# A planned attention + gated-FFN kernel: q projections interleaved, gate matmuls queued later, a longer landing time in the planner, final waits sorted

## The chip, the cores and the metric

The kernel runs on one core of one Trainium2 chip. Times are device microseconds (us) of that core. Engines: PE is the TensorE matmul, PEld its weight load, DVE VectorE, ACT ScalarE, POOL GpSimd, SP the engine that issues nearly all DMAs; "SPq" and "ACTq" are issues by a sequencer.

## The reference, cut to what matters

```python
x = A_x                                             # 1 x 2048 x 512, bf16
g = sigmoid((x * gate_w).sum(-1, keepdims=True))
a = memory_attention(x, wq, wk, wv, wo, beta)       # 32 heads of 16, 4 segments of 512 tokens
b = (relu(x @ W_gate) * (x @ W_up)) @ W_down        # 512 -> 1792 -> 512
return g * a + (1 - g) * b
# memory_attention, for each segment s: masked softmax attention inside the segment, mixed with
#   phi(q) @ M / (phi(q) @ z);  then  M += phi(k)^T v,  z += sum phi(k);   phi(t) = t+1 if t>0 else exp(t)
```

Segment 0 needs no memory. The first update of M is needed by segment 1.

## The kernel before

The kernel contains its own planner. Every operation is declared with what it reads, what it writes and a guessed duration. A list scheduler then takes, on each engine, the ready operation of the best priority (the lowest number first), and so fixes the engines' orders; semaphore waits follow from the dependences. So a guess never makes a result wrong. It decides which instruction stands before which, and in a fixed order an instruction that must wait holds up everything behind it on its engine. Two terms: a warm-up matmul works on zeros and nobody reads its result, it keeps PE busy until x has landed; wq is loaded in four contraction tiles of 128 rows, each by a DMA of its own.

```python
# place(): the planner's guess of when a DMA lands
self.dma_busy = max(self.dma_busy, issued) + op.nbytes / 340.0
op.end = self.dma_busy + (1700.0 if start < 16000.0 else 3200.0)
...
# start: warm-up matmuls, then x of segment 0 is transposed on PE
ds.append(dve(lambda e: e.memset(V.rl[:, 0, :], 0.0), 300, writes=["rl0"], name="warm0"))
xps, xcs = [warm(6, 0, 3)], []
...
# x of the later segments comes by DMA transposes, behind all weights but wo and wd
load_gu(0); load_gu(1); load_x(1); load gwb; load wo; load wd        # (shortened)
...
# gate: gw_pe turns gate_w, gq["pe"] is gmm (16 tiny matmuls); "flex" are 16 small copies of the gate
# for each segment (gexpT), on DVE or ACT
sc.queue(2, [gw_pe] + gq["pe"])
sc.queue(2, gq["flex"])
...
# keys of a segment: ek = exp(k) on ACT, ek = phi(k) on DVE, phik = ek transposed by a DMA, then the update
acts.append(act(lambda e, G=G: e.activation(V.ek[:, G, :], V.kT[:, G, :], ACT.Exp), ..., reads=[f"kT{G}"], writes=[f"ek{G}"], name=f"kexp{s}_{G}"))
sbs.append(dve(lambda e, G=G: e.tensor_tensor(V.ek[:, G, :], V.ek[:, G, :], V.ttmp[:, G % 2, :], ALU.min), ..., name=f"kphi{s}_{G}"))
sps.append(dma("sp", lambda e, G=G: e.dma_start_transpose(V.phik[:, :, G * 128:(G + 1) * 128], V.ek[:, G, :]), ..., name=f"kT2{s}_{G}"))
pes.append(pe(fn, mm(160, 8), reads=[f"phik{2 * hf}", f"phik{2 * hf + 1}"] + va(s), name=f"mu{s}_{hf}", ep=ep, role="w"))
...
# the end: SP waits for the last DMA of each of 16 semaphores
for i in range(sc.ndma):
    if sc.cnt[f"dma{i}"]:
        sc.prog["sp"].append(("wait", f"dma{i}", 16 * sc.cnt[f"dma{i}"]))
```

There is one `ek` for all segments. The first exp of `ek` of segment 1 (kexp1_0) therefore waits until the transposing DMA of segment 0 (kT20_0) has read the old one.

The softmax here doesn't subtract the row's maximum and nothing guards it: scores larger than these inputs give would overflow.

## Time and profile before

| | before |
|---|---|
| time, median of the first 3 runs | 275.39 us (275.25 to 275.47) |
| span of the profiled run | 273.4 us |
| first matmul | 1.24 us |
| PE idle before the quad at 36.02 us | 0.87 us |
| end of the last matmul to end of the span | 2.79 us |

From the page of the kernel before: the span, the busy time of each engine (share of the span, number of instructions), and the chain of work that ended last, by engine.

```profile
span 273.4 us, 5333 instructions
PE 263.7 (96%) x2122; PEld 115.8 (42%) x2157; DVE 206.3 (75%) x402; ACT 198.4 (73%) x205; POOL 120.6 (44%) x167
PE 90%; DMA 4%; issue 2%; ACT 1%; DVE 1%; ACTq 1%
```

PE is the bound. A gain must come from time in which PE stands still.

From the timeline of the kernel before (start, duration, engine, line, operation, tiles; in brackets the idle time just before and what ended it):

```profile
26.60 5.19 SPq L603 DMA_TRANSPOSE phik<-ek  x3
...
33.57 0.63 ACT L600 ACTIVATE ek<-kT 128x512 bf16<-128x512 bf16 x1 [1.84 <-DMA phik<-ek]
...
34.07 0.47 PEld L623 LDWEIGHTS psA<-vaug,phik 128*128 128x128 bf16 x8 [0.52 <-DMA phik<-ek]
34.07 0.65 PE L623 MATMUL psA<-vaug,phik 128*128 128x136 bf16 x8
...
34.11 1.86 ACT L682 ACTIVATE E<-psL 128x2048 bf16<-128x2048 f32 x1
...
36.02 0.40 PE L677 MATMUL psL<-qT,kp 32*128 32x256 bf16 x8 [0.87 <-ACT E L682]
```

The transposes of `ek` are issued from 26.60 us. ACT waits 1.84 us for the first of them to land before it may overwrite `ek`. The exp of the logits behind it starts only at 34.11. It frees the PSUM banks that the next logits ("quad", L677) need, and PE waits 0.87 us for them.

The start, from the same view, where the change interleaves:

```profile
6.93 0.17 PE L514 MATMUL psA<-ident,g 4*128 4x4 bf16 x1
7.11 0.13 PEld L580 LDWEIGHTS psA<-xT,wq 128*128 128x128 bf16 x2
7.14 1.09 PE L580 MATMUL psA<-xT,wq 128*128 128x512 bf16 x4
...
7.61 0.13 PEld L580 LDWEIGHTS psA<-xT,wq 128*128 128x128 bf16 x2 [0.37 <-DMA wq<-in_A_wq_dram]
```

The prediction reads these four q matmuls as 1.09 us in place of 0.86. 1.09 runs from the first start to the last end, and each record is 0.38 us long, while the starts lie 0.22 us apart. Four that wait for nothing read 1.02 us in the same view (from the timeline of experiment 2's run, e_ek2):

```profile
7.28 1.02 PE L580 MATMUL psA<-xT,wq 128*128 128x512 bf16 x4
```

So the late second half of wq cost PE 0.07 us here, though the weight load waited 0.37. Before these four PE waits for the small gate load; counted from start to start that cost 0.18 us (0.49 us after the last warm-up matmul, 0.31 in e_dma, where nothing is waited for).

### The profile page before, as it was taken

The numbers are of one execution on the slowest core, as the hardware profiler recorded it, in microseconds if no ns is written. First come the engines' busy times: TensorE is split into PE (matmuls) and PEld (weight loads), VectorE is DVE, ScalarE is ACT, GpSimd is POOL, SyncE is SP. The second block draws the span as 40 slices with busy tenths as digits, with TensorE's granted clock in tenths as the row PEclk, the third lists the DMA queues.
The fourth block names the chain that finished last, engine by engine and source line by source line (L and its number), as shares of the span: only waits on it lengthen the run. The fifth ranks groups of instructions, "written<-read, shape, count | busy, mean of one in ns | idle before, by whom it ended". The sixth has DMA issues, their size and how long they took to land.

```text
span 273.4 us, 5333 instructions
## 1 busy us (share of the span) xinstructions
PE 263.7 (96%) x2122; PEld 115.8 (42%) x2157; DVE 206.3 (75%) x402; ACT 198.4 (73%) x205; POOL 120.6 (44%) x167
## 2 busy tenths in 40 slices
PE   8999989999999999999999999999999999999995
PEld 4433333434444444443434444444344343434444
DVE  5599979899999799999698968687863338688200
ACT  3498696888877897798668779977677678784122
POOL 4004975687637483754444464324233424241000
DMA  6997952111001235200013111000012000000011
GB/s 194 334 337 195 304 101 57 42 36 45 0 2 38 61 78 95 59 22 0 2 20 73 46 38 37 23 2 0 2 38 60 20 19 22 1 2 0 0 41 38
DMA packets 31025, 17.01 MB, mean 62 GB/s; under 512 B 20760, under 2 KB 31000, under 8 KB 31000
## 3 DMA queue, kind: packets, MB, share of 16 engines
q1 hardware_dynamic: 30416, 16.14, 23.3%
q10 hardware_dynamic: 584, 0.53, 0.7%
q8 instruction: 17, 0.28, 0.4%
q14 instruction: 8, 0.07, 0.1%
HBM read 9.84 MB, written 2.10 MB: 44 GB/s over the span
## 4 chain that ended last, share of the span: by engine, by line
PE 90%; DMA 4%; issue 2%; ACT 1%; DVE 1%; ACTq 1%
PE psA L747 35%; PE psA L786 18%; PE psL L677 9%; PE psA L580 8%; PE psA L702 7%; PE psA L578 5%; PE psA L779 5%; DMA phik<-ek 3%; DMA g<-in_gate_w_dram 2%; PE psA L652 1%; PE psA L623 1%; ACT E L682 1%; ACTq L414 1%; PE psA L639 0%; DVE ek L602 0%
## 5 line engine op out<-in xcount | busy, mean ns | idle before, releaser
L682 ACT ACTIVATE E<-psL 128x2048 bf16<-128x2048 f32 x80 | 150.0, 1875 | 33.6 <-PE psL L677 32.9
L685 POOL TENSOR_SCALAR_AFFINE_SELECT E<-E 128x512 bf16<-128x512 bf16 x128 | 86.1, 690 | 125.2 <-ACT E L682 125.1
L747 PE MATMUL psA<-xT,wg 128*128 128x512 bf16 x213 | 57.2, 380 | 1.7 <-issue 1.7
L747 PE MATMUL psA<-xT,wu 128*128 128x512 bf16 x218 | 58.0, 380 | 0.7 <-issue 0.5
L786 PE MATMUL psA<-wd,hT 128*128 128x512 bf16 (+1 forms) x230 | 53.5, 367 | 0.9 <-issue 0.6
L758 DVE TENSOR_TENSOR hT<-psA,rl 128x512 bf16<-128x512 f32 x56 | 38.3, 685 | 12.0 <-PE psA L747 11.0
L677 PE MATMUL psL<-qT,kp 32*128 32x384 bf16 (+3 forms) x512 | 31.7, 301 | 0.9 <-ACT E L682 0.9
L786 PEld LDWEIGHTS psA<-wd,hT 128*128 128x128 bf16 x238 | 21.6, 98 | 23.2 <-issue 3.6
L747 PEld LDWEIGHTS psA<-xT,wu 128*128 128x128 bf16 x224 | 20.4, 98 | 25.5 <-issue 2.9
L707 DVE STREAM_TRANSPOSE Tn<-psA 128x512 f32<-128x512 f32 x32 | 21.6, 700 | 12.4 <-PE psA L702 12.1
L747 PEld LDWEIGHTS psA<-xT,wg 128*128 128x128 bf16 x224 | 19.6, 98 | 24.7 <-issue 4.5
L596 POOL TENSOR_SCALAR kp<-kT,pm 128x512 bf16<-128x512 bf16 x15 | 24.6, 1640 | 1.3 <-DVE kT L593 1.0
L755 ACT ACTIVATE rl<-psA 128x512 bf16<-128x512 f32 x27 | 16.1, 596 | 11.9 <-PE psA L747 11.0
L756 DVE TENSOR_SCALAR rl<-psA 128x512 bf16<-128x512 f32 x29 | 19.8, 684 | 5.4 <-PE psA L747 4.5
L677 PEld LDWEIGHTS psL<-qT,kp 32*128 32x128 bf16 x512 | 8.9, 92 | 33.1 <-ACT E L682 19.2
L702 PE MATMUL psA<-E,vaug 128*17 128x256 bf16 (+3 forms) x512 | 21.0, 300 | 0.0
L796 ACT ACTIVATE osb<-psA,omg 128x512 bf16<-128x512 f32 (+1 forms) x12 | 7.8, 651 | 15.3 <-PE psA L779 13.3
L580 PE MATMUL psA<-xT,wq 128*128 128x512 bf16 x60 | 15.8, 379 | 0.6 <-issue 0.5
L779 PE MATMUL psA<-wo,oT 128*128 128x512 bf16 (+1 forms) x66 | 16.0, 366 | 0.3 <-issue 0.3
L580 PE MATMUL psA<-xT,wk 128*128 128x512 bf16 x62 | 15.5, 379 | 0.2 <-issue 0.2
L578 PE MATMUL psA<-wv,xT 128*128 128x512 bf16 x62 | 15.1, 380 | 0.3 <-issue 0.3
L702 PEld LDWEIGHTS psA<-E,vaug 128*17 128x17 bf16 x512 | 10.5, 90 | 10.8 <-issue 2.3
(75 smaller groups left out, 237.9 us busy)
## 6 DMA issues: line engine op xcount, KB each, us to landing
out_dram<-osb SPq DMA_DIRECT2D x15, 128.0 KB, 1.7
wg<-in_B_W_gate_dram SPq DMA_DIRECT2D x8, 224.0 KB, 5.4
wu<-in_B_W_up_dram SPq DMA_DIRECT2D x8, 224.0 KB, 6.1
wd<-in_B_W_down_dram SPq DMA_DIRECT2D x1, 1792.0 KB
osb<-in_A_x_dram SPq DMA_DIRECT2D x12, 128.0 KB, 2.1
wk<-in_A_wk_dram SPq DMA_DIRECT2D x4, 128.0 KB, 5.0
wv<-in_A_wv_dram SPq DMA_DIRECT2D x4, 128.0 KB, 4.4
wo<-in_A_wo_dram SPq DMA_DIRECT2D x1, 512.0 KB, 5.4
```

Of the source, the lines that this page charges most:

```text
L578: ins = e.matmul(A(ep)[:, :], lhsT=V.xT[:, kt, tok + col * 128:tok + (col + 1) * 128], rhs=w[:, kt, :], start=(kt == 0), stop=(kt == KT - 1))
L580: ins = e.matmul(A(ep)[:, :], lhsT=w[:, kt, col * 128:(col + 1) * 128], rhs=V.xT[:, kt, tok:tok + 512], start=(kt == 0), stop=(kt == KT - 1))
L596: km = lambda e, G=G, p=p, ks=ks: e.tensor_scalar(V.kp[:, ks, :], V.kT[:, G, :], V.pm[:, p:p + 1], None, ALU.mult)
L677: ins = q.matmul(PL[:, jj, o:o + w], lhsT=V.kp[32 * jj:32 * jj + 32, kslot(s, n), 128 * j:128 * j + 128], rhs=V.qT[32 * jj:32 * jj + 32, q ...
L682: acts.append(act(lambda a, e=e: a.activation(V.E[:, e, :, :], PL[:, :, :], ACT.Exp, scale=SCALE), t_act(2048), reads=[f"bankL{b}" for b i ...
L685: pools.append(pool(lambda g, ap=ap: g.affine_select(out=ap, in_=ap, compare_op=ALU.is_ge, fill=0.0, base=0, pattern=[[0, 4], [1, 128]], c ...
L702: ins = q.matmul(A(ep)[32 * jj:32 * jj + 17, c:512], lhsT=V.vaug[:, s % 2, j, 8 * G + 2 * jj + p, :], rhs=V.E[:, e, jj, o:o + w], start=(j ...
L707: ds.append(dve(lambda e, p=p, ep=eps[p]: e.transpose(V.Tn[:, p, :], A(ep)[:, :]), t_dve(512), writes=[f"Tn{p}"], name=f"tr{s}_{G}_{p}", e ...
L747: ins = e.matmul(A(ep)[:, :], lhsT=w[:, kt, f * 128:(f + 1) * 128], rhs=V.xT[:, kt, c * 512:(c + 1) * 512], start=(kt == 0), stop=(kt == K ...
L758: evs.append(dve(lambda e, ep=eu, r=r, hs=hs: e.tensor_tensor(V.hT[:, hs, :], A(ep)[:, :], V.rl[:, r, :], ALU.mult), t_dve(512), reads=[f" ...
L779: ins = e.matmul(A(ep)[:, 0:c1 - c0], lhsT=V.oT[:, o0 + G, i * 128:(i + 1) * 128], rhs=V.wo[:, G, c0:c1], start=st_ and G == 0, stop=sp_ a ...
L786: ins = e.matmul(A(ep)[:, 0:c1 - c0], lhsT=V.hT[:, slots[f], i * 128:(i + 1) * 128], rhs=V.wd[:, f, c0:c1], start=st_ and f == f0, stop=sp ...
```

## The change

The intent: the first two q projections interleaved by contraction tile as wq lands; the first memory update planned later; the final waits in order of landing. The diff also queues the gate matmuls at a lower priority. Cut to its core (the lines that only follow from the splitting and from the shorter memset are left out):

```diff
-            op.end = self.dma_busy + (1700.0 if start < 16000.0 else 3200.0)
+            op.end = self.dma_busy + (1700.0 if start < 16000.0 else 5200.0 if start < 60000.0 else 3200.0)
...
-    ds.append(dve(lambda e: e.memset(V.rl[:, 0, :], 0.0), 300, writes=["rl0"], name="warm0"))
+    ds.append(dve(lambda e: e.memset(V.rl[:, 0, 0:128], 0.0), 130, writes=["rl0"], name="warm0"))
...
-    xps, xcs = [warm(6, 0, 3)], []
+    xps, xcs = [warm(5, 0, 3)], []
...
-    sc.queue(2, [gw_pe] + gq["pe"])
+    sc.queue(3, [gw_pe] + gq["pe"])
...
-            for k0 in range(0, KT, 2):
+            step = 1 if s == 0 and name == "q" and col < 2 else 2
+            for k0 in range(0, KT, step):
...
             pes = [p for k in "qkv" for p in pes if p.name[0] == k]
+            pes[:2 * KT] = [pes[h * KT + kt] for kt in range(KT) for h in range(2)]
...
-    for i in range(sc.ndma):
+    for i in sorted(range(sc.ndma), key=lambda i: sc.dma_end.get(i, 0.0)):
```

More of the change, by code (lines that the diff above doesn't have):

```diff
@@ L481, in fn @@
             for i in range(n):
-                ins = e.matmul(PL[:, b, :], lhsT=V.rl[:, 0, 0:128], rhs=V.rl[:, 0, :], start=True, stop=True)
+                ins = e.matmul(PL[:, b, :], lhsT=V.rl[:, 0, 0:128], rhs=V.rl[:, 0, 0:128].unsqueeze(1).to_broadcast([128, 4, 128]), start=True, stop=True)
             return ins
         return pe(fn, n * (427 if k == 0 else 260), reads=["rl0"], writes=[f"bankL{b}"], name=f"warm{k}")
-    xps, xcs = [warm(6, 0, 3)], []
+    xps, xcs = [warm(5, 0, 3)], []
     for i in range(4):
@@ L572, in pj @@
             ep = Epoch("proj")
-            for k0 in range(0, KT, 2):
+            step = 1 if s == 0 and name == "q" and col < 2 else 2
+            for k0 in range(0, KT, step):
                 def fn(e, k0=k0):
-                    for kt in (k0, k0 + 1):
+                    for kt in range(k0, k0 + step):
                         if tokmajor:
@@ L581, in fn @@
                     return ins
-                pes.append(pe(fn, mm(512, 2), reads=[f"{wname}{k0}", f"{wname}{k0 + 1}"] + xt(s), name=f"{name}{s}_{col}", ep=ep, role="w2" if k0 else "w"))
+                pes.append(pe(fn, mm(512, step), reads=[f"{wname}{kt}" for kt in range(k0, k0 + step)] + xt(s), name=f"{name}{s}_{col}", ep=ep, role="w2" if k0 else "w"))
             return ep
```

## The prediction

> **What bounds it.** TensorE. The page gives a span of 273.4 us with PE busy 263.7 (96%); the chain that ended last is 90% PE. The matmuls stay but for one warm-up matmul, so the change can only win from the 9.7 us in which PE is idle. A table of 5 us stretches shows where: 1.24 us before the first matmul, 2.7 us after the last, 0.2 us in 5 to 10 us, 0.87 us in 35 to 40 us, and elsewhere bits of 0.16 us where matmuls change shape. Those bits stay.
>
> **What the change does.**
> 1. First projections. The timeline shows PE waiting 0.60 us for the small gate-weight load (until 6.93), then 4 q matmuls taking 1.09 us because later wq tiles landed late (weight load waited 0.37 us, until 7.61), then 16 tiny gate matmuls. Four steady projection matmuls take 0.86 us. With q0 and q1 interleaved, PE has four matmuls to do before the late tiles are needed, and the gate matmuls, at lower priority, no longer stand in front. Saved: 0.25 us at the late tiles and 0.1 to 0.2 us at the gate load. Given back: both q tiles finish together, one DVE copy is 0.69 us, and q2 waits for the first. Net 0.2 us.
> 2. Warm-up: a shorter memset (0.27 us before), 5 in place of 6 matmuls. The transposes then wait only for x (landed about 3.65) and start 0.1 us earlier, but wq's landing gates the projections. Worth 0. The Trainium skill (TensorE: Matmul & The Clock Gate, section "The HAM clock gate") says the clock opens after about 3.4 us of a busy, free-running window; the trace agrees in kind (warm-up matmuls are recorded at 634 ns early, 379 ns from about 6 us). If fewer matmuls move that, it costs some tenths.
> 3. The planner's DMA time for starts from 16 to 60 us grows by 2 us. In the trace the first phik transposes, issued at 26.60, landed after 6.95 us. The old plan (about 4.9 us) put the first memory-update matmuls, and an exp of ek that overwrites what the DMA still reads, too early: PE waited 0.52 us, ACT 1.84 us; the next exp of the logits started only at 34.11 and PE sat idle 0.87 us before the quad at 36.02. The new plan (6.9 us) puts other ready work there. But every other DMA in that stretch (phik's median is 2.4 us) is now planned too late, and every later choice of the list scheduler can fall differently. I count 0.6 us gained, with noise of half a us either way.
> 4. Final waits sorted by landing: the last DMA issue is at 271.20, the last SP wait ends about 273.0, the span at 273.4. Waits already met cost 20 to 30 ns each. Worth 0.1 us.
>
> **Sum.** 0.2 + 0 + 0.6 + 0.1 = 0.9 us off 275.39: **274.5 us**, range 273.5 to 275.5. Chances: faster by over 2% 0.01, within 2% 0.98, slower by over 2% 0.01.
>
> **What would show it.** (1) the timeline at 6.8 to 10 us: no wait on wq tiles, gate matmuls after the first eight; (2) clock opening still near 6 us; (3) in the waits, the memory-update weight load and the ek exp no longer wait for the phik DMA, and PE is busy about 4.8 of 5 us in 35 to 40; (4) a shorter stretch from the last landing to the end.
>
> **What would make it wrong.** The new order loses elsewhere: exps (the quads wait on them) pushed behind gate copies or relu; DVE, saturated from 12 to 30 us, delays the first key copies; phik lands later still; a later clock opening.

## The result, and the profile after

| | before | after |
|---|---|---|
| time, median of 6 runs | 275.43 us (274.58 to 275.75) | 274.28 us (273.85 to 274.54) |
| ratio of fast runs | | 0.996, 95% interval 0.9943 to 0.9976 |
| span of the profiled run | 273.4 us | 272.6 us |
| first FFN matmul (L747, L749 after) | 18.85 us | 18.58 us |
| end of the last matmul to end of the span | 2.79 us | 2.56 us |

A ratio is the mean time of one kernel's fast runs over that of the other's of the same rounds, so it is not quite the ratio of the medians. The kernel before scatters from 274.58 to 276.65 us over all rounds; a difference of 0.3 us between two kernels is hardly resolved by time alone, and the traces have to decide.

The lines of the page after that answer to those above:

```profile
span 272.6 us, 5368 instructions
PE 268.2 (98%) x2156; PEld 115.6 (42%) x2156; DVE 206.0 (76%) x421; ACT 192.9 (71%) x182; POOL 123.2 (45%) x171
PE 94%; DVE 3%; DMA 1%; ACT 1%; issue 0%; DVEq 0%
```

PE seems busier by 4.5 us, in a run shorter by 0.8. Most of that is the records: none are missing here. The Trainium skill (Perfetto Trace Analysis, section "Identifying the Most-Contended Engine") calls matmul busy time a bad measure of how close a kernel is to its roofline, because pipelined matmuls look smaller in the trace, and names MFU (the share of the peak rate that was used) and weight-load busy time as better ones. In this pair the weight loads stand at 42% both times, so they do not see the change at all; the stalls in the timeline do.

The same stretch of the timeline after, and the gate copies (gexpT) that have moved into it:

```profile
22.64 0.38 DVE L546 COPY gexpT<-gexp 32x4 f32<-32x4 f32 x1
25.34 0.90 ACT L547 ACTIVATE gexpT<-gexp 32x4 f32<-32x4 f32 x4
26.80 0.75 DVE L546 COPY gexpT<-gexp 32x4 f32<-32x4 f32 x4
...
30.31 0.41 DVE L603 TENSOR_TENSOR ek<-ek,ttmp 128x512 bf16<-128x512 bf16 x1
...
30.75 1.22 SPq L604 DMA_TRANSPOSE phik<-ek  x1
...
39.17 1.15 ACT L601 ACTIVATE ek<-kT 128x512 bf16<-128x512 bf16 x2
```

The first transpose is now issued at 30.75 and lands at 33.69 us by its semaphore, 2.94 us later (6.95 us before). So it lands no sooner than before (33.55). Both times it comes behind the load of W_down, issued at 22.35 and 22.52 us, whose last semaphore update comes at 33.06 and 33.19; from 30 to 31 us the DMAs move 349 GB/s in both. What has moved is who needs it: the exp that overwrites `ek` runs at 39.17 (33.57 before), the first memory update at 40.5 (34.07). Nobody waits. In windows (busy us and number of instructions of PE, PEld, DVE, ACT, POOL; then the clock, DMA share and GB/s), 30 to 31 and 33 to 38 us read, before:

```profile
30.00:31.00 1.00, 1.00 (x7) 0.44 (x5) 1.00 (x2) 1.00 (x1) 1.00 (x2) 1.00 1.11 349
33.00:38.00 5.00, 3.94 (x37) 1.81 (x31) 4.37 (x9) 4.43 (x5) 4.40 (x6) 1.00 0.78 130
```

and after:

```profile
30.00:31.00 1.00, 1.00 (x6) 0.39 (x4) 1.00 (x4) 0.94 (x1) 0.00 (x0) 1.00 1.10 349
33.00:38.00 5.00, 5.00 (x33) 1.94 (x32) 4.17 (x10) 4.47 (x6) 4.43 (x6) 1.00 0.75 90
```

A sum over the two profiled runs: the first FFN matmul comes 0.27 us sooner, the stall of 0.87 us is gone, the tail is 0.23 us shorter, and two new idle spells of PE stand at 85.19 us (0.21, shown below) and 129.7 us (0.12). That makes -1.04 us where the span shows -0.85. What makes up the other 0.19 us was not tested.

```profile
85.19 0.59 PE L641 MATMUL psA<-Mbd,phiq 128*128 128x8 bf16 x16 [0.21 <-DVE phiq L592]
```

### The profile page after: what moved, and what is told of

Read it like the earlier page. It is cut to its first block, busy times and chain, and to the rows that moved or that the text cites. A ratio compares the mean times of both kernels' runs of the same rounds, so it can differ in the third digit from the quotient of the medians.

```text
span 272.6 us, 5368 instructions
## 1 busy us (share of the span) xinstructions
PE 268.2 (98%) x2156; PEld 115.6 (42%) x2156; DVE 206.0 (76%) x421; ACT 192.9 (71%) x182; POOL 123.2 (45%) x171
## 4 chain that ended last, share of the span: by engine, by line
PE 94%; DVE 3%; DMA 1%; ACT 1%; issue 0%; DVEq 0%
PE psA L749 36%; PE psA L788 18%; PE psA L581 10%; PE psL L679 9%; PE psA L704 7%; PE psA L579 5%; PE psA L781 5%; DMA hT<-in_A_x_dram 1%; PE psA L654 1%; PE psA L625 1%; DVE gexpT L546 1%; PE psL L490 1%; ACT E L684 1%; PE psA L641 1%; DVE hT L760 1%; PE psL L482 0%
## 5 line engine op out<-in xcount | busy, mean ns | idle before, releaser
L687 POOL TENSOR_SCALAR_AFFINE_SELECT E<-E 128x512 bf16<-128x512 bf16 x128 | 83.1, 667 | 116.1 <-ACT E L684 113.0
L749 PE MATMUL psA<-xT,wu 128*128 128x512 bf16 x224 | 59.8, 380 | 0.0
L749 PE MATMUL psA<-xT,wg 128*128 128x512 bf16 x224 | 59.5, 380 | 0.1
L788 PE MATMUL psA<-wd,hT 128*128 128x512 bf16 (+1 forms) x238 | 54.6, 367 | 0.0
L597 POOL TENSOR_SCALAR kp<-kT,pm 128x512 bf16<-128x512 bf16 x19 | 30.7, 1620 | 2.6 <-PE psL L679 1.2
L749 PEld LDWEIGHTS psA<-xT,wu 128*128 128x128 bf16 x224 | 20.4, 98 | 25.4 <-issue 3.1
L749 PEld LDWEIGHTS psA<-xT,wg 128*128 128x128 bf16 x224 | 19.9, 98 | 24.7 <-issue 3.7
L758 DVE TENSOR_SCALAR rl<-psA 128x512 bf16<-128x512 f32 x28 | 19.0, 680 | 3.6 <-PE psA L749 2.9
L581 PE MATMUL psA<-xT,wq 128*128 128x512 bf16 x64 | 16.5, 380 | 0.0
L581 PE MATMUL psA<-xT,wk 128*128 128x512 bf16 x64 | 16.4, 381 | 0.0
L797 DVE TENSOR_SCALAR osb<-psA,omg 128x512 bf16<-128x512 f32 x8 | 6.0, 746 | 12.9 <-PE psA L788 12.9
L798 ACT ACTIVATE osb<-psA,omg 128x512 bf16<-128x512 f32 (+1 forms) x9 | 5.8, 639 | 13.7 <-PE psA L781 13.3
```

What stands on the lines that cost most here:

```text
L581: ins = e.matmul(A(ep)[:, :], lhsT=w[:, kt, col * 128:(col + 1) * 128], rhs=V.xT[:, kt, tok:tok + 512], start=(kt == 0), stop=(kt == KT - 1))
L597: km = lambda e, G=G, p=p, ks=ks: e.tensor_scalar(V.kp[:, ks, :], V.kT[:, G, :], V.pm[:, p:p + 1], None, ALU.mult)
L687: pools.append(pool(lambda g, ap=ap: g.affine_select(out=ap, in_=ap, compare_op=ALU.is_ge, fill=0.0, base=0, pattern=[[0, 4], [1, 128]], c ...
L749: ins = e.matmul(A(ep)[:, :], lhsT=w[:, kt, f * 128:(f + 1) * 128], rhs=V.xT[:, kt, c * 512:(c + 1) * 512], start=(kt == 0), stop=(kt == K ...
L788: ins = e.matmul(A(ep)[:, 0:c1 - c0], lhsT=V.hT[:, slots[f], i * 128:(i + 1) * 128], rhs=V.wd[:, f, c0:c1], start=st_ and f == f0, stop=sp ...
```

## The experiments

Two ways of editing were used. "Planned anew" means that a part of the change is put in or left out and the planner runs again. "Order kept" means that the planner's order is written out again instruction for instruction, with one local edit, and only the waits are worked out anew (in e_warm6 the planner's guesses are left as they were, which comes to the same); such a run changes one thing and nothing follows from it by re-planning. "Planned at" is a time in the planner's own reckoning, got by running it. One of the six runs of e_iw was slow; its median counts it (277.58 us without), its ratio does not. All twelve runs gave correct results.

| run | what | median us | ratio to before of its rounds (95%) |
|---|---|---|---|
| e_sort | before + sorted waits | 275.33 | 1.0 (0.9981 to 1.002) |
| e_dma | before + constant | 276.41 | 1.0045 (1.0028 to 1.0061) |
| e_nodma | change without constant | 274.63 | 0.9985 (0.9967 to 1.0002) |
| e_ek2 | before's order, ek not overwritten | 274.28 | 0.9972 (0.9958 to 0.9987) |
| e_after2 | the change again | 274.03 | 0.9949 (0.9934 to 0.9963) |
| e_g | before + gate priority | 275.5 | 1.0002 (0.9988 to 1.0016) |
| e_gd | before + gate priority + constant | 274.27 | 0.9958 (0.9941 to 0.9975) |
| e_iw | before + interleaving + warm-up | 277.72 | 1.0078 (1.0061 to 1.0095) |
| e_best | e_gd's order + the rest | 273.66 | 0.9959 (0.9939 to 0.998) |
| e_oldstart | change's order, old start | 274.52 | 0.9978 (0.9964 to 0.9993) |
| e_warm6 | change's order, old warm-up | 274.42 | 0.998 (0.9964 to 0.9995) |
| e_x1 | change, constant for one load only | 274.02 | 0.9945 (0.9927 to 0.9964) |

### 1. The sorted waits alone (e_sort)

```diff
-    for i in range(sc.ndma):
+    for i in sorted(range(sc.ndma), key=lambda i: sc.dma_end.get(i, 0.0)):
```

> The kernel before with nothing but the final waits sorted by planned landing; no engine's order changes before the last store. My theory: the stretch from the end of the last matmul to the end of the span shrinks from 2.79 us to about 2.6 us, time 0.1 to 0.2 us shorter. Rival (the tail is only the last store's landing): no change, within 0.05 us.

The time does not resolve it (ratio 1.0). The traces do: from the last matmul's end to the end of the span it is 2.77 to 2.79 us in every fast profile with the waits unsorted (five), and 2.55 to 2.56 us in every one with them sorted (eight). Unsorted, SP waits for the last store and then goes through four more wait instructions (two semaphores each) that are long met, about 0.06 us each; sorted, the last store's is the last wait. So 0.22 us, and it is the tail alone.

The order of the kernel before, with no records missing:

```profile
span 274.2 us, 5368 instructions
PE 268.8 (98%) x2157; PEld 115.8 (42%) x2157; DVE 206.2 (75%) x402; ACT 198.4 (72%) x205; POOL 120.0 (44%) x167
```

The spells of 0.16 us that the first profile showed some 27 times are not there. And the stall is larger, as the transposes landed later (34.52 us, 33.55 in the first profile). From the timeline of this run:

```profile
34.55 0.63 ACT L600 ACTIVATE ek<-kT 128x512 bf16<-128x512 bf16 x1 [2.46 <-DMA phik<-ek]
...
35.06 0.65 PE L623 MATMUL psA<-vaug,phik 128*128 128x136 bf16 x8 [0.67 <-DMA phik<-ek]
...
37.00 0.40 PE L677 MATMUL psL<-qT,kp 32*128 32x256 bf16 x8 [0.86 <-ACT E L682]
```

So this stall is worth 0.87 us in one execution and 0.67 + 0.86 us in another of the same order.

### 2. What the stall hangs on: ek not overwritten, order kept (e_ek2)

```diff
+EK = V.amem[:, G, :] if s == 1 and G < 2 else V.ek[:, G, :]     # in exp, min and transpose of ek
+frozen(sc, drop=lambda o, p: o.name in ("kexp1_0", "kexp1_1") and p.name.startswith("kT20"))
```

`amem` is idle then; the second line keeps the order and drops the wait that is no longer needed.

> The kernel before in exactly its own order of instructions on every engine; the only change is that the first two exps of ek of segment 1 write into a buffer that is idle then, so ScalarE need not wait until the phik transposes of segment 0 have been read. Theory A (the stall of TensorE comes over ScalarE: exp of ek waits for the DMA, so the next exp of logits is late, so the next quad is late): ScalarE's 1.84 us wait is gone, the 0.87 us idle of TensorE before 36 us falls below 0.2, time 0.6 to 0.9 us shorter. Theory B (it comes over TensorE's own wait, the memory-update matmuls for phik): the idle moves to the memory-update matmuls at 34 us, and the time falls by less than 0.3 us.

Theory A holds. ACT, from the timeline of this run:

```profile
31.16 0.62 ACT L589 ACTIVATE phiq<-qT 128x512 bf16<-128x512 bf16 x1
31.68 0.62 ACT L600 ACTIVATE amem<-kT 128x512 bf16<-128x512 bf16 x1
32.20 1.87 ACT L682 ACTIVATE E<-psL 128x2048 bf16<-128x2048 f32 x1
```

The exp of the logits starts at 32.20 in place of 34.11, the quad at 35.10 in place of 36.02 without a wait, and PE has no idle spell over 0.06 us from its first matmul to its last. The wait of theory B is still in the trace (the weight load of the memory update waits 0.49 us for phik until 34.09), but PE has work until then. The time falls by 0.28%, 0.77 us (0.0028 x 275.01, the median of before in these rounds). With the order of the kernel before untouched, this one wait is worth more than half of what the whole change brings (0.40 and 0.51% in its two sets of rounds).

### 3. Which part of the change removed it: the constant (e_dma, e_nodma)

```diff
-            op.end = self.dma_busy + (1700.0 if start < 16000.0 else 3200.0)
+            op.end = self.dma_busy + (1700.0 if start < 16000.0 else 5200.0 if start < 60000.0 else 3200.0)
```

e_dma puts this line alone into the kernel before; e_nodma takes it alone out of the changed kernel. Both are planned anew.

> The kernel before with nothing but the planner's landing time of DMAs raised from 3.2 to 5.2 us for starts from 16 to 60 us. Theory as predicted (the larger constant moves the first memory update behind the landing and ends the 0.87 us stall of TensorE): 0.5 to 0.9 us shorter, ScalarE no longer waits for the phik transposes. Rival (the constant is not what ended the stall in the changed kernel; here the plan moves the first update only from 33.25 to 34.00 us, about when the transposes landed before): the wait for phik stays in part, and the time is within 0.3 us of before, or longer by what the new order costs.

> The changed kernel with the planner's old constant of 3.2 us. Theory as predicted: the stall before 36 us comes back and the time rises by 0.5 to 0.9 us over the changed kernel's 274.3, to 274.8 to 275.2. Rival (the new start of the plan already moves the first update: it is planned at 37.6 us here, 33.25 in the kernel before): no stall there, no wait for phik, time within 0.4 us of the changed kernel.

Alone, the constant makes the kernel slower by 0.45%. It does act on this stall as the prediction had it: ACT's wait for phik falls from 1.84 to 0.17 us, and PE idles only 0.21 us near 34.8 us. But the new plan puts two exps of ek between two exps of logits later on, and PE waits there (and 0.30 us more at 166.94 us):

```profile
34.30 0.63 ACT L600 ACTIVATE ek<-kT 128x512 bf16<-128x512 bf16 x1 [0.17 <-DMA phik<-ek]
...
68.72 0.40 PE L677 MATMUL psL<-qT,kp 32*128 32x384 bf16 x8 [1.19 <-ACT E L682]
```

Left out of the changed kernel, the stall before 36 us does not come back: PE is busy 5.00 of 5.00 us in 33 to 38 us. So in the changed kernel the constant is not what ends it. What comes in its place is a wait of the first projection of segment 1 for its x:

```profile
24.10 1.02 PE L581 MATMUL psA<-xT,wq 128*128 128x512 bf16 x4 [0.98 <-DMA xT<-in_A_x_dram]
```

These x transposes are issued from 15.1 to 19.1 us, behind the weights, and the last lands at 23.97 us. The Trainium skill (DMA: Bandwidth & Descriptors, section "Queues, rings and completion order") says that each DMA engine takes a queue's descriptors in ring order. The trace fits: 4.9 us from issue to landing for that one, against 2.5 us for an x transpose of the next segment in the same run (issued at 36.69 us, with little before it). The planner's 3.2 us had it landed at 23.0 us and the projection at 23.6. Another idle spell, 0.51 us at 122.4 us, stands in experiment 5's run too.

### 4. The gate priority (e_g, e_gd), and the interleaving with the warm-up (e_iw)

```diff
-    sc.queue(2, [gw_pe] + gq["pe"])
+    sc.queue(3, [gw_pe] + gq["pe"])
```

e_g is the kernel before with this line, e_gd with this line and the constant, e_iw with the interleaving and the warm-up alone; all planned anew. e_after2 is the changed kernel in the same rounds.

> The changed kernel again, as the measure for the other three of these rounds and for how far its own runs scatter. Ratio to before 0.996 as in its first rounds; no stall near 36 us; first FFN matmul at 18.0 to 18.7 us.

> The kernel before with one number changed: the priority of the gate matmuls' queue, 2 to 3. The planner then sets the first phik transpose at 29.8 us (25.9 before) and the first memory update at 37.6 us (33.25 before). Theory G (this line, not the DMA constant, ends the stall before 36 us): ScalarE does not wait for phik, no TensorE idle over 0.3 us in 33 to 40 us; 0.4 to 0.9 us shorter than before, unless TensorE arrives at segment 1's first projection before its x has landed (23.2 to 24.0 us so far), which would take part of it back there. Rival (the interleaving or the constant does it): the stall stays.

> The kernel before with the gate priority and the DMA constant changed, without the interleaving, the warm-up change and the sorted waits. Theory G plus constant (the constant's work is to plan segment 1's first projection after its x lands): no stall before 36 us and none at 24 us; time within 0.4 us of the changed kernel, about 0.2 us of that for the unsorted tail (2.78 us after the last matmul, 2.56 in the changed kernel). Rival (interleaving and warm-up carry the gain): within 0.3 us of before.

> The kernel before with the interleaved q projections and the shorter warm-up alone. The planner leaves the first memory update at 33.3 us. Theory G: the stall before 36 us stays (TensorE idle 0.7 to 1.5 us in 33 to 37 us); time within 0.5 us of before, as only some 0.2 us come from the start. Rival (the interleaving gives the gain): 0.8 us or more shorter than before.

In e_g the stall before 36 us is gone: PE is busy 5.00 of 5.00 us in 33 to 38 us and nobody waits for phik; the first transpose is issued at 30.64 and lands at 33.31 us.

```profile
33.00:38.00 5.00, 5.00 (x39) 1.93 (x32) 4.09 (x9) 4.47 (x6) 4.44 (x6) 1.00 0.81 96
```

So this line ends it, not by a planned landing time but by a detour. The 16 tiny gate matmuls run some 10 us later (at 20.25 us in e_g and 18.18 in the changed kernel, 8.07 before). Their 16 small copies, which filled an idle ACT from 8.9 to 14 us before, now stand on ACT and DVE at 22 to 28 us, in front of phi(k). The transposes are issued some 4 us later and land when they did before (33.31, 33.55 us), but the exp that overwrites ek is planned at 39.3 us in place of 31.3, long after the landing. The time is the same as before all the same (1.0002), since the new plan stalls elsewhere: 0.14 and 0.11 us of idle PE before the first and the third q matmul (see 6), 0.23 us at 24.09 us, where x of segment 1 had landed at 23.95, and 1.15 us at 73.37 us:

```profile
68.56 3.48 POOL L596 TENSOR_SCALAR kp<-kT,pm 128x512 bf16<-128x512 bf16 x2 [0.37 <-DVE kT L593]
...
72.00 1.22 POOL L685 TENSOR_SCALAR_AFFINE_SELECT E<-E 128x512 bf16<-128x512 bf16 x2
...
73.37 0.72 PE L702 MATMUL psA<-E,vaug 128*17 128x512 bf16 x16 [1.15 <-ACT gexpT L547]
```

The profile puts that last one down to ACT's copies just before it, but the program waits at that place for two things: ACT's 53rd instruction, a relu that ended at 70.95, and POOL's 52nd, the second mask of E, which ended at 73.22. So POOL held it. In front of the masks it had two maskings of kp, 3.48 us together, for which the planner had counted 0.68 us each (spans on POOL are rough, but the count of its semaphore comes to 52 only at 73.23).

With the constant added (e_gd) the last two are gone, PE has no idle spell over 0.06 us after its first matmul, and the ratio is 0.9958, within the changed kernel's scatter (0.9949 in the same rounds). Two numbers of the planner carry the gain, neither alone.

e_iw is slower by 0.78%, where "within 0.5 us" was expected. Its profile fell in a slow run (clock 0.95), so only the presence of waits is read from it: ACT still waits for phik (1.6 us) and PE 0.59 us at 36.5, and a new stall of 0.71 us stands at 116.6. What makes up the 2 us that it loses was not shown. The rival theory, that the interleaving alone gives the gain, falls.

### 5. What the constant does in the changed kernel (e_x1)

```diff
+            op.end = self.dma_busy + (1700.0 if start < 16000.0 else 5200.0 if op.name.startswith("ldx1") else 3200.0)
```

> The changed kernel with the larger landing time (5.2 us) planned for one load only, the x of segment 1; every other load is planned with 3.2 us as in the kernel before. Theory (what the constant does for the gain is to plan segment 1's first projection after its x lands, at 25.6 us in place of 23.6 us; the phik transposes do not need it once the gate matmuls are planned late): no idle of TensorE at 24 us (0.98 us there without the constant), no wait for phik, ratio to before 0.994 to 0.997 as in the changed kernel, unless the new order stalls elsewhere. Rival (the constant works on phik): a wait for phik comes back near 34 to 38 us.

The ratio is 0.9945. No wait for x at 24 us, none for phik. The first projection of segment 1 starts at 25.49 us, after x landed at 24.26. Of the idle spells left the largest is 0.52 us at 121.6 us. So what the constant brings to the changed kernel is the x of segment 1; the memory update, which it was meant for, does not need it.

### 6. The start: interleaving, gate load, warm-up (e_oldstart, e_warm6), and a version meant to beat both (e_best)

```diff
# e_oldstart: order of the changed kernel kept, on PE only
-  q0 q1 q0 q1 q0 q1 q0 q1 gwT ...
+  gwT q0 q0 q0 q0 q1 q1 q1 q1 ...
# e_warm6: order of the changed kernel kept; memset of 512 columns, six warm-up matmuls of plain rows
# e_best: order of e_gd kept; sorted waits, five warm-up matmuls, short memset, q0 q1 q0 q1 by pairs of tiles
```

> The changed kernel's order kept instruction for instruction, but the first small gate matmul put back before the q projections and q0, q1 done one after the other; nothing is planned anew. My prediction's step 1 (worth 0.2 us net): the time rises by about 0.2 us over the changed kernel; in the trace the first q matmul waits for the gate load, and the second half of q0 waits for wq, 0.1 to 0.4 us together, and the first FFN matmul starts that much later. Rival (the wq tiles and the gate load have landed by the time the warm-up ends): no wait, no change.

> The changed kernel's order kept instruction for instruction, with six warm-up matmuls and the longer memset as before; nothing is planned anew. My prediction's step 2 (worth 0): within 0.2 us of the changed kernel. Rival (the earlier start of the warm-up opens the clock sooner): the last warm-up matmul starts at 6.4 us on average as in the runs with six, against 5.4 to 6.6 in those with five, and the time rises by 0.2 to 0.5 us.

> A version meant to beat both: the order of the kernel with the gate priority and the DMA constant alone (no idle of TensorE over 60 ns after its first matmul), kept instruction for instruction, with the final waits sorted, five warm-up matmuls, the shorter memset, and the first two q tiles taken in turn by pairs of contraction tiles. Theory: 0.22 us less after the last matmul than that kernel and 0 to 0.2 us at the start: 273.8 to 274.1, ratio to before 0.994 to 0.995. Rival (all that counts is already in the changed kernel): 0.996 again.

In e_oldstart no wait for wq appeared: it had landed by 6.42 us, before the warm-up ended, and the eight q matmuls start at their steady 0.22 us. The gate load delays the tiny matmul before them by 0.06 us (0.37 us after the last warm-up matmul, in place of 0.31). In the 14 profiles the last wq tile landed at 6.03 to 7.51 us; the profile of the kernel before, from which the prediction took its 0.37 us, has the latest. But what counts is the landing against the end of the warm-up. Counted from start to start, the two waits cost 0.24 us in the kernel before, 0.06 in e_ek2 and in e_oldstart, and nothing in e_sort and e_dma. In e_g, where PE was at full speed from 4.9 us and the q matmuls were not interleaved, the third of them waited for wq and started 0.48 us after the second, 0.26 too late. So the interleaving saves nothing in some executions and some 0.3 us in others, and no times here resolve it.

The start is moved more by the clock. The first matmul recorded at full speed begins anywhere from 4.3 to 7.3 us in these profiles (with six warm-up matmuls 4.9 to 7.3, with five 4.3 to 7.2), and the first FFN matmul follows it: 17.94 us in e_after2, 18.58 in the first profile of the same kernel (full speed from 5.1 and 6.3 us). By time, e_oldstart and e_warm6 lie 0.2 to 0.3% above the changed kernel, but in other rounds, and their intervals overlap that of its first rounds (not quite that of its second): nothing was shown for or against either.

e_best has the best median, 273.66 us, and PE ends with no idle spell after the transposes of x. One of its six runs took 275.08, its ratio of 0.9959 is that of the changed kernel, and it is not shown to beat it.

## Why the prediction was right or wrong

The time was right: 274.5 predicted, 274.28 measured, in a range of 273.5 to 275.5. The sum was right for reasons that were in part wrong. The three terms came out near what was predicted in the first pair of profiles (0.27, 0.54 and 0.23 us for 0.2, 0.6 and 0.1), and two of them by luck: the 0.54 came by another line than the one named, and the 0.27 from an execution in which the gate load and wq were late.

1. **Where PE stands still.** The 0.87 us before 36 us was the right place, and e_ek2 shows its mechanism as the prediction had it (DMA, exp of ek, exp of logits, quad). The "bits of 0.16 us where matmuls change shape" were wrong: they were missing matmul records. Complete records of the same order show none, so of the 9.7 us that the page called idle, some 4.3 us never were (27 spells of 0.16 us).
2. **Step 3, the cause.** "The planner's DMA time ... The new plan (6.9 us) puts other ready work there" is the step that failed. The constant alone does shorten ACT's wait, to 0.17 us, but it gave +0.45% (e_dma), and without it the stall stays away (e_nodma). The gate priority, which the prediction used only for the start, moved the exp of ek from 33.6 to 39.5 us, behind a landing that hardly moved (e_g); the constant then kept segment 1's first projection from running into its x (e_nodma, e_x1). The size, 0.6 us net with half a us of noise, was near: 0.87 us gained, 0.33 us lost again at 85 and 130 us in the first profile.
3. **Step 1, the start.** The 0.25 us for the late tiles was mis-sized: 1.09 was set against 0.86, where four matmuls that wait for nothing read 1.02 in the same view, so it was 0.07. The gate load cost 0.18, as predicted. Together 0.24 us, in that execution, and its wq landed latest of 14; with the same start the two waits cost 0 to 0.06 us in four others. No time measured here resolves it from zero.
4. **Step 2, the warm-up.** Worth 0 was predicted, and nothing else was shown. That a moved opening of the clock would blur it was rightly feared: it moves the start by more than the whole of steps 1 and 2.
5. **Step 4, the tail.** 0.1 us predicted, 0.22 us measured, in every trace. The term was mis-sized: I took 20 to 30 ns for each wait already met, as the trace records them, but from one such wait to the next it is about 60 ns, and there were four.
6. **The noise of a new plan** was named as the risk and counted as half a us. It is larger: single parts of the change gave 0.9945 to 1.0078.

## What to carry to other kernels

In a kernel whose order comes from a planner, ask of every changed number what it moves in the plan, not what it was meant to move: here a queue priority meant for the first microseconds shifted an exp at 33 us, and a constant meant for one DMA helped another. When parts of a change work only together, test them alone and in pairs, and keep the order fixed when one wait is to be priced by itself. When the profile names who ended a wait, check in the program what was waited for. Before explaining short gaps in an engine's trace, count its records.

## What the Trainium skill lacked or had wrong

- TensorE: Matmul & The Clock Gate, section "The HAM clock gate": it gives the opening of the clock at about 4 us of activity, within 500 ns from run to run. Here PE was busy from 1.04 or 1.24 us on (with a break of up to 0.5 us in some runs with five warm-up matmuls), and the first matmul at full speed began at 4.3 to 7.3 us in 14 profiles, 3.3 to 6.2 us after the first matmul. Its free-running window allows such a spread; its 500 ns do not.
- Perfetto Trace Analysis: the page does not say that matmul records can be missing from a profile. Why they were was not tested. The first profile here had 2122 matmuls for 2157 weight loads, and its PE busy time was 263.7 us where a complete profile of the same order had 268.8.
- DMA: Bandwidth & Descriptors: it has no figure for a DMA transpose behind a filled queue. The same phik transpose took 2.4 us from issue to landing at its median and 6.95 us behind the weight loads, 7.8 us in another execution (26.72 to 34.52) and 9.1 us in e_dma (25.21 to 34.28).
- I found no page with the cost of a wait instruction on SP whose semaphores are already met (a sequencer's read of a semaphore's value is another thing): about 0.06 us each here, 0.22 us for four of them at the end of the kernel.
